# Block-sparse attention and an MLP on one core: the first pair's loads in runs of three tokens, and a new written-out order

## The chip, the cores and the metric

The kernel runs on one core of a Trainium2 chip. The metric is the device time of one execution in microseconds (us); the time given for a kernel is the median of its runs. PE is the engine of matrix products, DVE the vector engine, ACT the one of activations, POOL the general one, and SP issues most of the DMAs.

## What is computed

Four batches of 8 heads attend over 768 tokens with 64 elements per head. Each head's keys are 12 blocks of 64 tokens. A token attends to its own block and to the three blocks of its past whose mean key has the largest product with its query, causally. The heads' results, side by side, are the rows x of an MLP: 3072 rows, 512 to 2048 elements, gelu in its tanh form, and back to 512. In short (f32 in and out):

```python
k_rep = k.reshape(B, H, n_blocks, block, D).mean(axis=3)
gate_scores = np.einsum('bhsd,bhnd->bhsn', q, k_rep)        # only past and own blocks count
top_idx = np.argsort(gate_scores, axis=-1)[..., -3:]
mask = (block of key in top_idx, or own block) & (pos_q >= pos_k)
attn = softmax(where(mask, scale * q @ k.T, -1e9)) @ v
x = attn.transpose(0, 2, 1, 3).reshape(B * S, H * D)
out = gelu_tanh(x @ w_in) @ w_out
```

## The kernel before

**Staging.** Heads are worked in pairs, 16 pairs p = 0..15, four to a batch. Per batch there is an attention stage (heads) and an MLP stage: s1, the first product (L1115) with its gelu (L1127), and s2, the second (L1315 for batch 0; L1365 with sums on DVE, L1302 and L1414, in the others, which trades additions for an eighth of the products). The last batch has its first product in seven such products too (L1204). Attention of batch b + 1 is interleaved with the MLP of batch b, so that only batch 0's attention has no matrix products of an MLP beside it.

**Batch 0, a pair.** Keys and queries come in with tokens on the partitions and must be turned. `load` (L387) fetches 192 KB per head and tensor on the SP queue; the eight semaphores of DMAs go round, so that an issue can wait for the landing of an earlier one. Pair 0 has a loader of its own, `load_0` (L421): keys on the SP queue, queries on the ACT queue, four pieces of 96 KB each (half of the tokens of one head), with every token's 64 floats, 256 bytes, on another partition. `turn` makes three f32 products or transposes per half of the tokens: for pairs 0 and 1 (`KSUM`) the keys go through a product (L538) with `identk`, the identity of 128 columns with two more that hold ones for either block of a 128-token chunk, so that block sums fall out beside the turned keys; all others are transposes (L541). `turned` copies the result out of PSUM (the copies' own lines: L360 on DVE, L356 on ACT, L358 on POOL). `ksb_h` makes the sums' two-head form: from the product's extra columns by one multiplication with `bmask` (L588), or by a reduction (L576) and a multiplication (L582). The gate (L680) is four products in column strips of 32 (`tile_position`); DVE then makes the selection: transpose (L696), causal addition (L703), one max8 per group (L712), comparison (L713), and `madd`, the additive mask (L717). PE turns the mask (L749) and DVE copies it beside the queries, where it is 12 more rows of the contraction of S^T (L856: a key part of 64 rows and one with the mask's). ACT takes the exponential (L875), POOL clears what lies behind the diagonal (L901), PE multiplies with the values and a column of ones (L924), DVE divides (L942, L943), and PE turns the result into x (L981). Pair 0 has its gate in two halves, the second with `ksbx`. `cast_v` and `q16` make f16 of values and queries on POOL.

**Batches 1 to 3.** Keys and queries are transposed by DVE in 32 x 32 blocks (L557), cast to f16 (keys on DVE or POOL, queries on DVE or ACT), and the rest is as above (L1039 scores, L1052 exponential, L1066 causal, L1078 values, L961 and L962 division).

**Constants and weights.** POOL and DVE write the constants (L274 to L302, L470 to L510). POOL issues w_in as two DMAs of 1 MB (L453) once the values of pair 3 have landed (L451), then w_out. L1560 is a DMA on the SP queue that waits for w_in and holds later loads back.

**Order.** A table sets everything: each step is an `Op` with its possible engines, and `run` emits them in the list `ORDER`, on the engine that `ENGINE` names (else the first that the step lists), in the buffers that `BUFFER` deals out:

```python
for n in ORDER:
    op = self.ops[n]
    for kind, key in op.takes:
        if key not in self.buf:
            self.buf[key] = self.kinds[kind][0][next(picks)]
    op.emit(engine.get(n, next(iter(op.engines))))
```

The order in the list is the order in which each engine issues; the waits follow from the data. Steps of `warm` are products with zeros (L1517) that keep PE busy where it would stand.

Of the kernel before, what the change touches and what calls it, by code (L numbers as in the profile page):

```python
# [8 lines left out]
FP32 = mybir.dt.float32  # L9
# [219 lines left out]
def kernel(  # L229
# [9 lines left out]
    nc = tc.nc  # L239
# [1380 lines left out]
```

## Time and profile before

| | |
|---|---|
| Median of 3 runs | 253.68 us (253.64 to 253.81) |
| Profiled execution | 254.11 us |
| its span | 252.4 us |
| PE busy | 244.2 us, 97% |
| DVE, ACT, POOL busy | 188.6, 178.5, 86.8 us |
| DMA | 130927 packets, 32.62 MB, 129 GB/s over the span |
| Granted PE clock | 1.0 in all slices |
| First product of the first MLP (L1115) | at 38.40 us |

The span is what the profiler saw between first and last instruction, 1.71 us less than that execution's time. Times in the trace count from the span's start. In its rows a name is a tile or a tensor (buffer numbers left out) and the shape is partitions x elements; `DVE` behind an arrow is the engine that ended the wait. A matmul in f32 shows as two records, a transpose as one. G, XS and TS are large buffers that lend room to batch 0's loads and f16 tiles (so `G<-in_q_dram` is a load of queries, `XS<-bank` a copy of turned keys or of a mask).

### The profile page before, as it was taken

What the parts mean: (1) busy time and instruction counts of PE and PEld (TensorE: products, weight loads), DVE (VectorE), ACT (ScalarE), POOL (GpSimd) and SP (SyncE); (2) the same over time, 40 slices, a digit from 0 to 9 for tenths busy, and PEclk for the clock granted to TensorE, in tenths of its full rate; (3) what the DMA queues carried; (4) which work ended last, traced back from release to release, by engine and by line L of the source; (5) the groups of instructions that cost most, each with busy time, mean ns of one, the idle gap of its engine ahead of it and who ended that gap; (6) DMA issues with size and microseconds to landing.
All of it is one profiled execution on the core that took longest, in us unless ns stands there. A gap on an engine that the chain in (4) does not pass through costs nothing.

```text
span 252.4 us, 6423 instructions
## 1 busy us (share of the span) xinstructions
PE 244.2 (97%) x2483; PEld 170.4 (68%) x2483; DVE 188.6 (75%) x533; ACT 178.5 (71%) x225; POOL 86.8 (34%) x169
## 2 busy tenths in 40 slices
PE   7898999999999999999999999999999999999993
PEld 5665786555546666555778887656778887666883
DVE  2799863031869999999898977999775785687954
ACT  2577877546799999767899897757998927667300
POOL 8766860002135587240066644420244500000000
PEclk9999999999999999999999999999999999999999
DMA  8999599999999895999998996351601250020024
GB/s 153 219 207 184 88 211 180 214 151 160 141 153 130 155 198 93 146 176 181 167 204 145 223 154 114 88 118 42 166 4 24 41 180 20 3 84 0 4 92 158
DMA packets 130927, 32.62 MB, mean 129 GB/s; under 512 B 124528, under 2 KB 126928, under 8 KB 130896
## 3 DMA queue, kind: packets, MB, share of 16 engines
q1 hardware_dynamic: 126160, 27.62, 64.7%
q0 software_dynamic: 3136, 4.19, 10.0%
q10 hardware_dynamic: 1600, 0.39, 0.8%
q8 instruction: 19, 0.31, 0.6%
q14 instruction: 12, 0.10, 0.1%
HBM read 27.26 MB, written 6.29 MB: 133 GB/s over the span
## 4 chain that ended last, share of the span: by engine, by line
PE 91%; DVE 4%; DMA 2%; issue 1%; ACTq 1%; ACT 0%; DVEq 0%
PE wide L1115 27%; PE bank L1365 22%; PE wide L1039 11%; PE bank L1315 8%; PE bank L1078 6%; PE wide L1204 5%; PE wide L856 3%; PE bank L680 2%; PE bank L924 2%; DMA G<-in_q_dram 2%; PE bank L541 1%; PE bank L749 1%; PE bank L981 1%; DVE sel L712 1%; DVE sel L713 1%
## 5 line engine op out<-in xcount | busy, mean ns | idle before, releaser
L1115 PE MATMUL wide<-xT,w_in 128*128 128x384 f16 x416 | 74.1, 326 | 0.0
L1052 ACT ACTIVATE ats<-wide 128x896 f16<-128x896 f32 x72 | 62.0, 913 | 3.6 <-PE wide L1039 1.3
L1127 ACT ACTIVATE G<-wide 128x768 f16<-128x768 f32 x52 | 42.0, 809 | 27.0 <-PE wide L1115 25.3
L1115 PEld LDWEIGHTS <-w_in 128*128 128x128 f16 x416 | 39.9, 98 | 26.8 <-issue 1.3
L1066 POOL TENSOR_SCALAR_AFFINE_SELECT ats<-ats 128x256 f16<-128x256 f16 x72 | 31.3, 450 | 58.1 <-ACT ats L1052 57.8
L1039 PE MATMUL wide<-qT,kT 76*128 76x512 f16 (+3 forms) x192 | 38.6, 305 | 0.0
L557 DVE STREAM_TRANSPOSE s<-sd 128x768 f32<-128x768 f32 x24 | 23.2, 970 | 13.7 <-DMA sd<-in_k_dram 11.5
L1365 PE MATMUL bank<-w_out,G 128*128 128x256 f16 x216 | 31.9, 272 | 0.0
L1365 PEld LDWEIGHTS <-G 128*128 128x128 f16 x288 | 27.2, 98 | 5.2
L1315 PE MATMUL bank<-w_out,G 128*128 128x512 f16 x96 | 28.1, 379 | 0.0
L1414 DVE TENSOR_TENSOR osb<-bank,osb 128x512 f32<-128x512 f32 (+1 forms) x38 | 22.2, 594 | 7.0 <-PE bank L1365 6.5
L1039 PEld LDWEIGHTS <-kT 76*128 76x128 f16 x192 | 17.3, 97 | 10.6 <-issue 0.5
L875 ACT ACTIVATE ats<-wide 128x1024 f16<-128x1024 f32 (+3 forms) x24 | 21.0, 916 | 4.7 <-PE wide L856 4.6
L1078 PEld LDWEIGHTS <-ats 128*128 128x128 f16 x504 | 21.8, 97 | 3.6 <-POOL ats L1066 0.2
L358 POOL CAST kT<-s 64x768 f16<-64x768 f32 x23 | 19.5, 846 | 14.0 <-DVE s L557 13.2
L1078 PE MATMUL bank<-v,ats 128*128 128x65 f16 x504 | 24.1, 194 | 0.0
L1365 PEld LDWEIGHTS <-XS 128*128 128x128 f16 x216 | 20.0, 97 | 4.8
L1365 PE MATMUL bank<-TS,XS 128*128 128x256 f16 x144 | 22.8, 272 | 0.0
L358 POOL CAST v<-vsd 128x768 f16<-128x768 f32 x13 | 10.7, 828 | 30.9 <-DMA vsd<-in_v_dram 22.2
L356 ACT CAST qT<-s 64x768 f16<-64x768 f32 x21 | 17.4, 827 | 0.3
L962 DVE TENSOR_TENSOR xn<-bank,zr 128x384 f16<-128x384 f32 x24 | 13.4, 558 | 0.8
L712 DVE MAX8 sel<-sel 128x8 f32<-128x12 f32 x160 | 13.3, 157 | 0.6
(118 smaller groups left out, 350.3 us busy)
## 6 DMA issues: line engine op xcount, KB each, us to landing
out_dram<-osb SPq DMA_DIRECT2D x23, 256.0 KB
vsd<-in_v_dram SPq DMA_DIRECT2D x26, 192.0 KB
sd<-in_k_dram SPq DMA_DIRECT2D x48, 96.0 KB
sd<-in_q_dram SPq DMA_DIRECT2D x48, 96.0 KB
w_in<-in_moe_w_in_dram POOLq DMA_DIRECT2D x2, 1024.0 KB, 11.3
w_out<-in_moe_w_out_dram POOLq DMA_DIRECT2D x2, 1024.0 KB, 18.5
G<-in_q_dram SPq DMA_DIRECT2D x4, 192.0 KB
G<-in_k_dram SPq DMA_DIRECT2D x4, 192.0 KB
```

The source lines that it names most:

```text
L358: nc.gpsimd.tensor_copy(out=out, in_=in_)
L557: nc.vector.transpose(out=T[key + "T32", p], in_=T[key, p].rearrange("p t j -> p (t j)"))
L875: nc.scalar.activation(out=T["at", u][:, :, 0:n], in_=plan.buf[("st",) + u].rearrange("p (h w) -> p h w", h=2)[:, :, 0:n], func=AF.Exp, bi ...
L1039: nc.tensor.matmul(st[:, x:e], kT16[i][h][0:76, s0:s0 + 128], qT16[i][h][0:76, s0 + (x - cb):s0 + (e - cb)], start=True, stop=True)
L1052: nc.scalar.activation(out=T["at", u][:, 0:n], in_=plan.buf[("st",) + u][:, 0:n], func=AF.Exp, bias=0.0, scale=SCALE)
L1066: nc.gpsimd.affine_select(out=dg, in_=dg, compare_op=ALU.is_ge, fill=0.0, base=0, pattern=[[0, 2], [1, 128]], channel_multiplier=-1)
L1078: nc.tensor.matmul(pvv[:, qc, 0:65], at[:, cb + (qc - jc) * 128: cb + (qc - jc + 1) * 128], v16[i][:, jc, h, :], start=(gi == 0 and jc == ...
L1115: nc.tensor.matmul(hps[:, 512 * e:512 * e + HALF], w_in16[:, ci, (2 * j + e) * 128: (2 * j + e + 1) * 128], T["xT", b][:, ci, HALF * h:HAL ...
L1127: nc.scalar.activation(out=G[:, :, h, j, :], in_=plan.buf["hps", b, j, h].rearrange("p (e w) -> p e w", e=2)[:, :, 0:HALF], func=AF.Gelu_a ...
L1315: nc.tensor.matmul(plan.buf["ops", b, ti], G[:, f % 2, 2 * ti // NC, f // 2, ti % (NC // 2) * 128:ti % (NC // 2) * 128 + 128], w_out16[:, ...
L1365: nc.tensor.matmul(dst[:, HD * h:HD * h + HD], FACT[m][0][:, j, t * 128:(t + 1) * 128], FACT[m][1][:, j, :], start=(clear and j == 0), sto ...
L1414: nc.vector.tensor_tensor(out=dst(), in0=src(), in1=other(), op=ALU.add)
```

## The change

1. **Pair 0's loads.** Each partition takes three consecutive tokens of a head, one run of 768 bytes instead of three of 256. The tile is seen as `p (c h) d`, a head's half as three columns of tokens.
2. **Pair 0's turning.** A half of keys or queries is six f32 products in place of three, one per head and token column, each into 64 of the 128 output partitions (`tile_position=(0, 64 * h)`). `identk` becomes 3 x 134 columns: three identities, each with six columns that mark which block a token lies in; keys take 134 columns, queries 128. The copies put the tokens back in order (`p (w c) -> p c w`).
3. **Block sums.** `KSUM` is empty. Pair 0's sums are a reduction over the three columns of six, then the multiplication with `bmask`; pair 1's keys are now transposed, and summed by a reduction over 64 like pairs 2 and 3.
4. **Engines.** For batch 0, `cast_v`, `q16` and one kind of constants (`ones`) may run on DVE or ACT too. `ENGINE` in batch 0: the first copy of pair 0's queries, its first mask copy, both key copies of pair 1 and the first of pair 2 go from DVE to ACT, the second of pair 2 from ACT to DVE; the casts of the values of pairs 2 and 3 and the first `ones` go from POOL to DVE. Later: four key casts POOL to DVE, six query casts and three other copies ACT to DVE, all net.
5. **Order.** `ORDER` and `BUFFER` are new over the whole kernel. The numbers of useful products from batch 1 on are the same (416 of L1115, 504 of L1365, 192 of L1039, 504 of L1078); the warm-up products fall from 37 to 34. On the SP queue the first piece of pair 1's keys now stands ahead of pair 0's four pieces of keys; on the ACT queue the exponential's table load stands between the two halves of pair 0's queries. On PE the start is: queries' first half, keys' first half, keys' second half, first gate, queries' second half, pair 1's first queries, second gate, first masks (before: queries' first half, keys' first half, queries' second half, first gate, keys' second half). On DVE, pair 3's query copies now come ahead of its keys' copies and sums. On POOL the cast of pair 1's values stands ahead of the causal clearings.

The core of the diff (the lists are left out):

```diff
-    KSUM = (0, 1)
+    KSUM = ()
+    RUN = (0,)
...
-    identk = const.tile([128, 130], FP32, name="identk")
-    ident32 = identk[:, 0:128]
+    ident32 = const.tile([128, 128], FP32, name="ident32")
     make_identity(nc, ident32)
+    identk = const.tile([128, 3, 134], FP32, name="identk")
+    inblk = identk[:, :, 128:134]
+    nc.gpsimd.memset(inblk, 1.0)
+    nc.gpsimd.affine_select(
+        out=inblk, in_=inblk, compare_op=ALU.is_ge, fill=0.0, base=0,
+        pattern=[[1, 3], [-64, 6]], channel_multiplier=3)
+    nc.gpsimd.affine_select(
+        out=inblk, in_=inblk, compare_op=ALU.is_ge, fill=0.0, base=63,
+        pattern=[[-1, 3], [64, 6]], channel_multiplier=-3)
+    nc.vector.tensor_copy(out=identk[:, :, 0:128], in_=ident32.unsqueeze(1)
+                          .to_broadcast([128, 3, 128]))
...
                         (nc.sync if eng == SP else nc.scalar).dma_start(
-                            out=T[key, 0][:, 3 * a:3 * a + 3, hh, :],
+                            out=T[key, 0][:, 6 * hh + 3 * a:
+                                          6 * hh + 3 * a + 3],
                             in_=SRC[key][0, hh, HALF * a:HALF * a + HALF]
-                            .rearrange("(c p) d -> p c d", p=128))
+                            .rearrange("(p c) d -> p c d", c=3))
...
         ld["v16", p] = add(
-            {POOL: 0.85}, emit,
-            [ld["v", p], old],
+            {POOL: 0.85, DVE: 0.56, ACT: 0.84} if b == 0 else {POOL: 0.85},
+            emit, [ld["v", p], old],
...
+                    n = 134 if key == "k" else 128
+                    for h in range(2):
+                        nc.tensor.matmul(
+                            w[64 * h:64 * h + 64, c * n:(c + 1) * n],
+                            T[key, p][:, 6 * h + 3 * a + c],
+                            identk[:, c, 0:n], start=True, stop=True,
+                            tile_position=(0, 64 * h))
...
                 copy(eng, dst()[:, a * HALF:(a + 1) * HALF].rearrange(
-                    "p (c w) -> p c w", w=128),
+                    "p (w c) -> p c w" if p in RUN else "p (c w) -> p c w",
+                    c=3),
...
+                    half = slice(6 * a, 6 * a + 6)
+                    w = plan.buf["wk", p, a]
+                    nc.vector.tensor_reduce(
+                        out=ks[:, half],
+                        in_=w[:, 0:402].rearrange(
+                            "p (c w) -> p w c", w=134)[:, 128:134]
+                        if p in RUN else w[:, 0:HALF].rearrange(
+                            "p (n w) -> p n w", w=64),
+                        op=ALU.add, axis=AXL.X)
                     for x in into:
                         nc.vector.tensor_tensor(
-                            out=x[:, :, 6 * a:6 * a + 6].rearrange(
-                                "p h (c b) -> p h c b", b=2),
...
+                            out=x[:, :, half], in0=bmask[:, :, 0:6],
+                            in1=ks[:, half].unsqueeze(1).to_broadcast(
+                                [128, 2, 6]), op=ALU.mult)
...
-            q16s = ([add({POOL: 0.85}, q16(0, S), qcs, pr + 0.1)] if p else
+            q16s = ([add({POOL: 0.85, DVE: 0.56, ACT: 0.84}, q16(0, S), qcs,
+                         pr + 0.1)] if p else
                     [add({DVE: 0.33}, q16(a, HALF), [qcs[a]], pr - 0.1)
                      for a in range(2)])
```

More of the change, by code (lines that the diff above doesn't have):

```diff
@@ L382, in first @@
                     "p (t j) -> p t j", j=32))
+            if key != "v" and p in RUN:
+                T[key, p] = sd.rearrange("p c h d -> p (c h) d")
             part(0)
         def part(n):
+            if key != "v" and p in RUN:
+                nc.sync.dma_start(
+                    out=T[key, p][:, 6 * n:6 * n + 6].rearrange(
+                        "p (a c) d -> p a c d", c=3),
+                    in_=SRC[key][b, 2 * hp + n].rearrange(
+                        "(a p c) d -> p a c d", p=128, c=3))
+                return
             if not dve:
@@ L500, in consts, with emit_p @@
         for i in range(NB):
-            def emit_p(_, i=i):
-                nc.gpsimd.memset(v16[i][:, :, :, 64:65], 1.0)
-                nc.gpsimd.memset(madd[i], 0.0)
+            def emit_p(eng, i=i):
+                on = nc.vector if eng == DVE else nc.gpsimd
+                on.memset(v16[i][:, :, :, 64:65], 1.0)
+                on.memset(madd[i], 0.0)
                 if i < HP - 1:
-                    nc.gpsimd.memset(mT2[i][:, 0:128], 0.0)
+                    on.memset(mT2[i][:, 0:128], 0.0)
                 for h in range(2):
-                    nc.gpsimd.memset(qT16[i][h][64:76, 0:128], 0.0)
-            c_E["ones", i] = add({POOL: 1.3}, emit_p, [], prio=-45 + 10 * i)
+                    on.memset(qT16[i][h][64:76, 0:128], 0.0)
+            c_E["ones", i] = add({POOL: 1.3, DVE: 0.8}, emit_p, [],
+                                 prio=-45 + 10 * i)
     def fill(i, after):
@@ L534, in emit @@
                 for c in range(3):
-                    src = T[key, p][:, 3 * a + c].rearrange(
-                        "p h d -> p (h d)")
-                    if key == "k" and p in KSUM:
-                        nc.tensor.matmul(w[:, c * 130:(c + 1) * 130], src,
-                                         identk, start=True, stop=True)
-                    else:
-                        nc.tensor.transpose(w[:, c * 128:(c + 1) * 128], src,
-                                            ident32)
+                    if p not in RUN:
+                        nc.tensor.transpose(
+                            w[:, c * 128:(c + 1) * 128],
+                            T[key, p][:, 3 * a + c].rearrange(
+                                "p h d -> p (h d)"), ident32)
+                        continue
+                    n = 134 if key == "k" else 128
[5 more added lines that the diff above has]
+                            tile_position=(0, 64 * h))
             return emit
@@ L563, in pre @@
             for a in range(2):
-                t = add({PE: 0.71 if p in KSUM else 0.34}, turn("k", a),
+                t = add({PE: 0.69 if p in RUN else 0.34}, turn("k", a),
                         [ld["k", p] if p else ld["k", 0, a]], pr,
-                        takes=("pre", ("wk", p, a)))
+                        takes=("pre", ("wk", p, a)), mode=3 * (p in RUN))
                 kts.append(t)
@@ L649, in pre @@
             for a in range(2):
-                t = add({PE: 0.34}, turn("q", a),
+                t = add({PE: 0.66 if p in RUN else 0.34}, turn("q", a),
                         [ld["q", p] if p else ld["q", 0, a]], pr,
-                        takes=("pre", ("wq", p, a)))
+                        takes=("pre", ("wq", p, a)), mode=3 * (p in RUN))
                 qts.append(t)
```

33 lines of the change are left out of this document (7 added, 26 removed), and 311 rows, old and new, of tables (BUFFER, ENGINE, ORDER).

## The prediction

> **What bounds the kernel now.** I read the page's totals and its chain first, then the busy time of each engine by stage, then the timeline of the first 42 us.
>
> ```profile
> span 252.4 us, 6423 instructions
> PE 244.2 (97%) x2483; PEld 170.4 (68%) x2483; DVE 188.6 (75%) x533; ACT 178.5 (71%) x225; POOL 86.8 (34%) x169
> PE 91%; DVE 4%; DMA 2%; issue 1%; ACTq 1%; ACT 0%; DVEq 0%
> ```
>
> The profiled execution took 254.11 us, 1.71 more than its span; the median of the runs, 253.68, lies 0.43 below it. PE is busy for 97% of the span, and 91% of the chain that ended last is PE. So a gain must come from the 8 us in which PE stands still, or from PE work taken out. The stages (each row: stretch, length, then busy time and count for PE, PEld, DVE, ACT and POOL; PE's clock, DMA share, GB/s) show where those 8 us are:
>
> ```profile
> 0.00:4.70 4.70, 3.63 (x17) 2.40 (x17) 1.01 (x15) 1.49 (x2) 3.70 (x19) 1.00 0.65 131
> 4.70:7.20 2.50, 1.74 (x15) 1.35 (x14) 1.07 (x4) 0.48 (x1) 2.32 (x8) 1.00 1.35 220
> 7.20:11.00 3.80, 3.06 (x41) 2.31 (x42) 2.77 (x12) 1.31 (x3) 3.55 (x8) 1.00 1.39 218
> 11.00:31.20 20.20, 18.57 (x307) 13.73 (x303) 18.46 (x77) 16.28 (x22) 12.83 (x23) 1.00 0.94 163
> 31.20:38.40 7.20, 7.15 (x147) 5.93 (x148) 5.02 (x14) 5.76 (x8) 4.16 (x7) 1.00 1.13 212
> 38.40:60.00 21.60, 21.60 (x147) 12.87 (x145) 5.27 (x10) 12.44 (x16) 1.23 (x2) 1.00 1.21 180
> 80.00:100.00 20.00, 19.96 (x252) 12.99 (x250) 18.85 (x50) 19.72 (x26) 14.63 (x27) 1.00 0.83 141
> 122.00:156.00 34.00, 34.00 (x411) 27.61 (x409) 29.94 (x58) 31.65 (x39) 17.68 (x32) 1.00 1.02 171
> ```
>
> From 38.4 us on PE is full: a new order there can lose, hardly gain. Ahead of it PE is short of work while pair 0's data comes in (to 7.2), between the gates of pair 0's halves (7.2 to 11), and while DVE makes the selections of batch 0 one after another (18.46 of 20.20 busy). Warm-up matmuls count as busy there, so that PE's true slack is larger than its row says. What the first 38 us lose or gain the end keeps, since nothing behind them has room.
>
> **The change part by part.** *Loads and turning of pair 0, up to its first gate.*
>
> ```profile
> 2.46 4.15 DMA G<-in_q_dram
> 3.00 1.28 ACT L822 ACT_TABLE_LOAD   x1 [3.00 <-issue]
> 4.79 0.52 PE L541 MATMUL bank<-identk,G 128*128 128x128 f32 x3
> 5.15 0.83 PE L538 MATMUL bank<-identk,G 128*128 128x130 f32 x6
> 6.74 0.52 PE L541 MATMUL bank<-identk,G 128*128 128x128 f32 x3 [0.76 <-DMA G<-in_q_dram]
> 7.19 0.16 PEld L680 LDWEIGHTS bank<-s,ksb 128*32 128x32 f32 x8 [0.17 <-issue]
> 7.19 0.32 PE L680 MATMUL bank<-s,ksb 128*32 128x64 f32 x8
> 11.48 1.61 PE L538 MATMUL bank<-identk,G 128*128 128x130 f32 x12
> DMA packets 5216, 1.31 MB, mean 218 GB/s; under 512 B 5216, under 2 KB 5216, under 8 KB 5216
> GB/s 349 334 364 349 213 61 0 0 0 0 0 0 0 0 0 152 243 394 394 425 394 273 364 455 425 304 304 319 379 303 379 228 91 0 0 0 0 0 91 212
> ```
>
> The row of 5216 packets is the DMA view from 7 to 13 us: loads in 256-byte pieces run at 218 GB/s. The last row, from the same view at 247.5 to 250.2 us, is the nearest with long packets (stores): slices of 300 to 455. For 768-byte pieces I take 330, between 218 and that row's common values; the ends are 218 and 425. Pair 0's keys and queries are eight pieces of 98 KB, 786 KB: at 218 GB/s 3.6 us, and the last landed at 6.61 (2.46 + 4.15), so that data flowed from about 3.0. Afterwards the SP queue first issues a 197-KB piece of pair 1's keys in the old form (0.90 us of traffic), and the ACT queue puts the table load of 1.28 between pair 0's two halves of queries, which delays the second half but not the first. Sharing the engines evenly, the first half of queries (0.60) is in at 4.2 and that piece of pair 1 at 4.5; the two halves of keys follow at 5.1 and 5.7.
>
> A half is now turned by six products instead of three, each into half of the columns. A product in f32 shows as two records. If the two column halves run side by side, a block takes what three full ones do: 0.83 by the row at 5.15; taken 0.8. If one runs after the other, it is the row of twelve: 1.61. The gate, four column strips, eight records of 64 columns in 0.32, speaks for side by side: at the same 1.61/12 for 130 columns they would take 0.53 in turn. Afterwards PE turns the first queries (4.2 to 5.0), both halves of keys (5.1 to 5.9, 5.9 to 6.7), then the gate: 6.7 for 7.19, **-0.5**. Ends: loads at 425 GB/s and blocks of 0.7 give a gate at 6.4 (-0.8); loads at 218 with blocks of 0.8 one at 7.4 (+0.2); blocks in turn are the first rival.
>
> The Trainium skill, "TensorEngine Tiling (Array Packing)", section "Tiling Modes", has it that tiles in different columns work in parallel, but also that a change of the tiling mode drains the engine, and that column tiling shuts out the f32 transpose. By it the side-by-side value would stand, and the sum with it, less a drain at each change; the trace has 0.17 us of idle weight loading ahead of the first gate, which agrees in kind.
>
> *From the first gate to the second.*
>
> ```profile
> 9.73 0.21 DVE L717 SCALAR_TENSOR_TENSOR madd<-sel,ownm 128x48 f16<-128x48 f32 x1
> 9.86 0.16 DVE L588 TENSOR_TENSOR ksbx<-bmask,bank 128x12 f32<-128x12 f32 x1
> 10.32 0.29 DVE L360 COPY XS<-bank 128x256 f16<-128x256 f16 x1 [0.30 <-PE bank L749]
> 10.98 0.28 DVE L696 STREAM_TRANSPOSE sel<-bank 128x96 f32<-128x96 f32 x1
> ```
>
> Between the first selection and the second gate's transpose DVE makes block sums (0.16), waits 0.30 for the masks on PE, and copies the mask (0.29). The new order turns the second half of keys before the first gate, so that the sums precede the selection, and gives the mask copy to ACT: 0.16 + 0.30 + 0.29, **-0.7**. What is late next is the second gate itself, behind pair 1's first queries on PE (0.5): then -0.2, the upper end.
>
> *DVE's stretch to pair 3's selection (10.98 to 31.19).*
>
> ```profile
> 12.56 0.16 DVE L588 TENSOR_TENSOR ksb<-bmask,bank 128x12 f32<-128x12 f32 x1
> 12.63 0.55 DVE L360 CAST XS<-bank 128x384 f16<-128x384 f32 x1
> 16.45 0.55 DVE L576 TENSOR_REDUCE ks<-bank 128x6 f32<-128x384 f32 x1
> 24.34 0.17 DVE L582 TENSOR_TENSOR ksb<-bmask,ks 128x12 f32<-128x12 f32 x1
> 28.53 0.35 DVE L696 STREAM_TRANSPOSE sel<-bank 128x160 f32<-128x160 f32 x1 [0.83 <-PE bank L680]
> 30.91 0.28 DVE L717 SCALAR_TENSOR_TENSOR madd<-sel,ownm 128x120 f16<-128x120 f32 x1
> 31.11 0.55 DVE L360 COPY xT<-bank 128x768 f16<-128x768 f16 x1
> ```
>
> Out: two key copies net (1.10), and the wait of 0.83, because pair 3's query copies now precede its keys' sums. In: pair 1's two sums, 0.16 each, become a reduction and a product, 0.55 + 0.17: +1.12. Together -0.8. Pair 1's turning on PE falls from 1.61 to about 1.0, hidden behind DVE; without that cover it would be worth -0.6. New waits are likely where DVE and PE now need copies from ACT; POOL's cast of pair 1's values stands ahead of its selects and waits for that load, and the products with values queue behind them. I take 0.6 of the 0.8 for that: **-0.2**, ends -0.8 and +0.8. The cast of pair 2's values now stands on DVE between pair 3's selection and its mask copy, where the xT copy of 0.55 stood; a cast of that size takes about 0.54 (below): **0**.
>
> *ACT in batch 0.*
>
> ```profile
> 13.62 0.48 ACT L356 COPY s<-bank 128x384 f32<-128x384 f32 x1 [0.69 <-PE bank L541]
> 33.08 1.94 ACT L875 ACTIVATE ats<-wide 128x1024 f16<-128x1024 f32 x2 [0.61 <-PE wide L856]
> ```
>
> ACT takes in net three copies of about 0.48 and the mask copy. It has 3.9 us free of 20.2 up to 31.2, which covers most; behind pair 3's mask it still waits for PE (0.61). I take one copy that comes between exponentials: **+0.4**, ends 0 and +1.2 (the first three on the path, and no more room).
>
> *Weights.*
>
> ```profile
> 26.63 1.66 POOL L453 DMA_DIRECT2D w_in<-in_moe_w_in_dram  x2 [0.35 <-issue]
> w_in<-in_moe_w_in_dram POOLq DMA_DIRECT2D x2, 1024.0 KB, 11.3
> 38.40 0.65 PE wide L1115 x4
> 41.10 0.57 SPq L1560 DMA_DIRECT2D after_in<-w_in  x1
> ```
>
> The second half of w_in is there at 41.1, 13.6 after an issue at about 27.5; with a median of 11.3 for two the first took 9.0 and came at 35.6. L1115 begins at 38.4 and by the sum at 37.4, so the weights cap the gain only at 2.8. Their issue waits for pair 3's values, at the end of the same SP queue; shorter loads ahead can only bring that forward. **0**.
>
> *Batches 1 to 3.*
>
> ```profile
> L358 POOL CAST kT<-s 64x768 f16<-64x768 f32 x23 | 19.5, 846 | 14.0 <-DVE s L557 13.2
> 56.15 0.54 DVE L360 CAST kT<-s 64x768 f16<-64x768 f32 x1
> ```
>
> Four key casts go from POOL (0.85) to DVE (0.54), six query casts from ACT to DVE: 5.4 us more on DVE in all. PE's products are the same in number. With PE full this is worth nothing while DVE keeps ahead; taken **+0.2**, ends 0 and the third rival.
>
> The sum: -0.5 - 0.7 - 0.2 + 0.4 + 0.2 = -0.8; 254.11 becomes 253.3 for a profiled execution, and the median 253.68 becomes **252.9**.
>
> **The rivals.** *Column halves in turn (slower).* A block of six takes 1.61 and the queries' about 1.5; PE, not the loads, then sets the gate: 4.2 + 1.5 + 1.6 + 1.6 = 8.9, +1.7 for -0.5, and the rest of the sum as above: +1.4, 255.1. It decides when a block takes over 1.1 us: then three blocks end after 7.5 and the other terms (-0.3) are used up. Against it stands the gate's row, for it that no 64-column strip is in the trace.
>
> *ACT takes the place of DVE (no change).* All moved copies stand ahead of exponentials: +1.2 for +0.4, the gain is gone, 253.7.
>
> *The later order stalls PE (slower).* From 80 to 100 us DVE is busy 18.85 and ACT 19.72 of 20: if a third of the 5.4 us more on DVE reaches PE through late casts or sums, it is +1.8 for +0.2, in all +0.8: 254.5. For it: those rows; against: 122 to 156, where DVE has 4 us free and PE stands nowhere. It decides from 1.0 us of new idle time on PE behind 38.4.
>
> *Longer pieces gain little.* If the price is mostly by bytes, and under half of the step from 218 to 330 is had, 768 bytes run at about 267 GB/s: the keys land at 5.4 and 6.1, the gate stands at 7.0, and the sum is -0.5: 253.2. Against it only the stores' row. The Trainium skill, "DMA: Bandwidth & Descriptors", section "Why small descriptors are slow (HBM only)", gives three fixed cycles beside eight of data for 256 bytes, by which 768 bytes would need 27 in place of 33; an estimate of 18% from that page, and that 267.
>
> *All covers hold.* Loads and blocks at the good end (-0.8), the second gate -0.7, DVE's -0.8, no price on ACT or later: -2.3, 251.4.
>
> **How the numbers follow.** Forecast 0.38, all covers 0.08, little by longer pieces 0.10, halves in turn 0.12, ACT 0.12, later stalls 0.20. This kernel's runs tell about 0.2%, 0.5 us, from no change. Little by longer pieces sits at that edge and is split: faster 0.38 + 0.08 + 0.05 = 0.51, the same 0.12 + 0.05 = 0.17, slower 0.12 + 0.20 = 0.32. The range runs from all covers, 251.4, past the later stalls to 254.8, and leaves out the halves in turn and the tails, some 0.2. The likeliest case by itself spans 252.0 to 253.2.
>
> **What would show it.** Right: pair 0's pieces of 98 KB landing 0.30 apart, blocks of twelve records in 0.7 to 0.9, the first gate by 6.9, the second gate's transpose near 9.8, pair 3's selection ending about 29.8, and the first L1115 near 37.4 with PE full behind it. Wrong: blocks over 1.1; a gate after 7.5; L1115 later than 38.4; or L1115 earlier and new idle time on PE in the stages of batches 1 to 3, which the forecast puts at 0.2.

## The result: 251.94 us for 253.75

The changed kernel took 251.94 us (median of 4 runs, 251.45 to 252.62), the kernel before 253.75 beside it (4 runs): a ratio of 0.9934 with an interval of 0.9909 to 0.9958. Run again later, it took 251.74 (5 runs), 0.9918 (0.9906 to 0.9931). So the gain is 1.8 to 2.1 us. The forecast was 0.8 (252.9); the measured times lie inside its range of 251.4 to 254.8. The profiled execution is the slowest of the first four, 252.62 us with a span of 250.9.

The page of the changed kernel:

```profile
span 250.9 us, 6484 instructions
PE 245.2 (98%) x2504; PEld 170.7 (68%) x2504; DVE 194.9 (78%) x551; ACT 173.8 (69%) x220; POOL 82.2 (33%) x161
PE 94%; DVE 4%; issue 0%; DVEq 0%
```

PE's share of the chain rose from 91% to 94%. The stages of the changed kernel, with the columns of the prediction:

```profile
10.20:29.06 18.86, 18.30 (x303) 13.38 (x301) 17.69 (x78) 16.43 (x25) 11.13 (x21) 1.00 0.86 166
31.20:38.40 7.20, 7.20 (x137) 5.70 (x134) 4.68 (x12) 6.47 (x8) 4.42 (x7) 1.00 1.12 205
80.00:100.00 20.00, 20.00 (x252) 12.86 (x250) 18.38 (x48) 17.50 (x23) 13.08 (x24) 1.00 0.63 111
```

The stretch from the second gate's transpose to the end of pair 3's selection is the first row: 18.86 us, where it was 20.21 (10.98 to 31.19), with DVE busy for 17.69 and not 18.46. From 31.2 on PE has no idle time (before, 0.05 us up to 38.4). The timeline shows where the steps now lie:

```profile
4.38 3.50 PE L565 MATMUL bank<-identk,G 128*64 128x128 f32 x36
7.80 0.32 PE L699 MATMUL bank<-s,ksb 128*32 128x64 f32 x8
8.05 0.88 PE L565 MATMUL bank<-identk,G 128*64 128x128 f32 x12
8.79 0.21 DVE L722 TENSOR_TENSOR sel<-sel,cgate 128x48 f32<-128x48 f32 x1
9.45 0.21 DVE L732 TENSOR_TENSOR sel<-sel,sel 128x48 f32<-128x48 f32 x1
10.20 0.28 DVE L715 STREAM_TRANSPOSE sel<-bank 128x96 f32<-128x96 f32 x1
26.59 0.91 DVE L722 TENSOR_TENSOR sel<-sel,cgate 128x120 f32<-128x120 f32 x1
28.78 0.28 DVE L736 SCALAR_TENSOR_TENSOR madd<-sel,ownm 128x120 f16<-128x120 f32 x1
36.51 0.81 PE L1135 MATMUL wide<-xT,w_in 128*128 128x384 f16 x4
38.98 0.57 SPq L1580 DMA_DIRECT2D after_in<-w_in  x1
```

The first gate came later, at 7.80 for 7.19. All the rest came earlier: the second gate's transpose by 0.8, the end of pair 3's selection (29.06) by 2.1, the first product of the MLP by 1.7, the end of the span by 1.5. (In the timeline that product starts at 38.24 before; the 38.40 given ahead is its row in the chain, where it starts when the product ahead of it has ended.) So the loads and the turning lost time, and DVE's way through the selections won it. The same way in the kernel before holds what the prediction did not look at:

```profile
7.69 1.87 POOL L494 TENSOR_SCALAR_AFFINE_SELECT G<-G 64x768 f16<-64x768 f16 x2
7.93 0.71 DVE L703 TENSOR_TENSOR sel<-sel,cgate 128x48 f32<-128x48 f32 x1
9.11 0.51 DVE L713 TENSOR_TENSOR sel<-sel,sel 128x48 f32<-128x48 f32 x1
16.83 0.83 POOL L358 CAST v<-G 128x768 f16<-128x768 f32 x1 [2.00 <-DMA G<-in_v_dram]
17.04 0.65 DVE L582 TENSOR_TENSOR ksb<-bmask,ks 128x12 f32<-128x12 f32 x1
21.42 1.00 POOL L901 TENSOR_SCALAR_AFFINE_SELECT ats<-ats 128x256 f16<-128x256 f16 x2 [1.91 <-ACT ats L875]
21.81 0.75 DVE L713 TENSOR_TENSOR sel<-sel,sel 128x120 f32<-128x120 f32 x1
22.37 0.87 POOL L358 CAST v<-TS 128x768 f16<-128x768 f32 x1
22.66 0.72 DVE L717 SCALAR_TENSOR_TENSOR madd<-sel,ownm 128x120 f16<-128x120 f32 x1
38.24 0.81 PE L1115 MATMUL wide<-xT,w_in 128*128 128x384 f16 x4
```

These are rows of the kernel before. The first two DVE operations take 0.21 each in the changed kernel; the one at 17.04 takes 0.17 elsewhere in the same trace, the last two 0.28. Each long one stands beside a POOL operation. Nine such operations between 7 and 31 us cost the kernel before 3.4 us more than their short forms; in the changed kernel six cost 1.6. (Counted are the operations with two inputs in SBUF that take over 0.06 more than their shortest form.) The difference of 1.8 is the size of the gain, which proves nothing by itself. Theory A: POOL stretches DVE's short operations, and the new order and engines win by keeping them apart. Theory L: the loads in runs of three win. A third question, W, came from PE's rate during pair 0's turning.

### The profile page after: what moved, and what is told of

The parts are those of the page before. It is cut to its first block, busy times and chain, and to the rows that moved or that the text cites. A ratio compares the mean times of both kernels' runs of the same rounds, so it can differ in the third digit from the quotient of the medians.

```text
span 250.9 us, 6484 instructions
## 1 busy us (share of the span) xinstructions
PE 245.2 (98%) x2504; PEld 170.7 (68%) x2504; DVE 194.9 (78%) x551; ACT 173.8 (69%) x220; POOL 82.2 (33%) x161
## 4 chain that ended last, share of the span: by engine, by line
PE 94%; DVE 4%; issue 0%; DVEq 0%
PE wide L1135 27%; PE bank L1385 22%; PE wide L1059 11%; PE bank L1335 8%; PE bank L1098 6%; PE wide L1224 6%; PE wide L876 3%; PE bank L699 2%; PE bank L1537 2%; PE bank L944 2%; PE bank L1001 1%; PE bank L565 1%; PE bank L558 1%; PE bank L769 1%; DVE sel L731 1%; DVE sel L722 1%
## 5 line engine op out<-in xcount | busy, mean ns | idle before, releaser
L1135 PE MATMUL wide<-xT,w_in 128*128 128x384 f16 x416 | 75.0, 326 | 0.0
L1059 PE MATMUL wide<-qT,kT 76*128 76x512 f16 (+3 forms) x192 | 38.4, 305 | 0.0
L1385 PE MATMUL bank<-w_out,G 128*128 128x256 f16 x216 | 33.7, 272 | 0.0
L1335 PE MATMUL bank<-w_out,G 128*128 128x512 f16 x96 | 29.2, 379 | 0.0
L1098 PEld LDWEIGHTS <-ats 128*128 128x128 f16 x504 | 22.7, 98 | 4.5 <-issue 0.3
L1098 PE MATMUL bank<-v,ats 128*128 128x65 f16 x504 | 24.9, 194 | 0.0
L1385 PE MATMUL bank<-TS,XS 128*128 128x256 f16 x144 | 22.1, 272 | 0.0
L367 POOL CAST kT<-s 64x768 f16<-64x768 f32 x19 | 16.3, 862 | 9.3 <-DVE s L585 8.0
L365 ACT CAST qT<-s 64x768 f16<-64x768 f32 x15 | 12.4, 825 | 0.2
```

Of the source, the lines that this page charges most:

```text
L367: nc.gpsimd.tensor_copy(out=out, in_=in_)
L1059: nc.tensor.matmul(st[:, x:e], kT16[i][h][0:76, s0:s0 + 128], qT16[i][h][0:76, s0 + (x - cb):s0 + (e - cb)], start=True, stop=True)
L1098: nc.tensor.matmul(pvv[:, qc, 0:65], at[:, cb + (qc - jc) * 128: cb + (qc - jc + 1) * 128], v16[i][:, jc, h, :], start=(gi == 0 and jc == ...
L1135: nc.tensor.matmul(hps[:, 512 * e:512 * e + HALF], w_in16[:, ci, (2 * j + e) * 128: (2 * j + e + 1) * 128], T["xT", b][:, ci, HALF * h:HAL ...
L1335: nc.tensor.matmul(plan.buf["ops", b, ti], G[:, f % 2, 2 * ti // NC, f // 2, ti % (NC // 2) * 128:ti % (NC // 2) * 128 + 128], w_out16[:, ...
L1385: nc.tensor.matmul(dst[:, HD * h:HD * h + HD], FACT[m][0][:, j, t * 128:(t + 1) * 128], FACT[m][1][:, j, :], start=(clear and j == 0), sto ...
```

## The experiments

All times are medians beside the kernel before, which took 253.8 in each group.

**The operations by themselves.** The kernel has no part of the computation.

> This kernel leaves the whole computation out and writes zeros; it has five stages. In each DVE runs the operations of a selection five times over, alone (stage 1), beside ACT copies (2), beside POOL's causal selects (3), beside POOL's casts (4) and beside POOL's memsets (5); at the end of each stage PE, idle until then, runs a train: 40 pairs of f32 products in column halves (1), 40 full f32 products (2), 40 full f16 products (3), 15 full f16 and then 40 pairs in column halves (4), 15 full f16 and then 40 full f32 (5). Theory A (POOL's work stretches DVE's short operations): the additive, comparing and multiplying operations that read only SBUF take 0.17 to 0.28 in stages 1 and 2 and 0.5 to 0.9 in stages 3 and 4, while the transpose, the reduction and the copy out of PSUM and the max8 stay at 0.34, 0.55, 0.55 and 0.16 in all. Rival: the long ones seen in the traces come from ACT, DMA or data, and all stages agree within 0.05. For PE: if column halves are slow by themselves, pairs are 0.21 apart through all of stage 1 and in stage 4, and full products 0.11 per record; if PE only starts slowly, every train begins at twice its later distance for about 3.5 us, whatever its form, and stage 4's column halves, after 3.2 us of full products, run at 0.11 per pair.

It was executed once. The groups by line of DVE follow: first the stage with nothing beside it (4.2 to 19.7 us), then beside POOL's selects (40.9 to 58.6), beside its casts (64 to 79) and beside its memsets (82.6 to 98.2):

```profile
L89 DVE CAST o<-src 128x384 f16<-128x384 f32 x5 | 1.8, 360 | 0.2
L78 DVE SCALAR_TENSOR_TENSOR madd<-sel,own 128x120 f16<-128x120 f32 x5 | 1.4, 283 | 0.2
L75 DVE TENSOR_TENSOR sel<-gm,mx 128x120 f32<-128x120 f32 x5 | 1.4, 283 | 0.2
```

```profile
L78 DVE SCALAR_TENSOR_TENSOR madd<-sel,own 128x120 f16<-128x120 f32 x5 | 3.2, 646 | 0.2
L68 DVE TENSOR_TENSOR gm<-gx,cg 128x120 f32<-128x120 f32 x5 | 1.8, 368 | 0.2
```

```profile
L78 DVE SCALAR_TENSOR_TENSOR madd<-sel,own 128x120 f16<-128x120 f32 x3 | 2.6, 855 | 0.1
L89 DVE CAST o<-src 128x384 f16<-128x384 f32 x4 | 2.3, 580 | 0.1
L75 DVE TENSOR_TENSOR sel<-gm,mx 128x120 f32<-128x120 f32 x3 | 1.5, 503 | 0.1
L66 DVE STREAM_TRANSPOSE gx<-src_ps 128x160 f32<-128x160 f32 x4 | 1.3, 334 | 0.0
L74 DVE MAX8 mx<-gm 128x8 f32<-128x12 f32 x9 | 1.0, 161 | 0.1
```

```profile
L89 DVE CAST o<-src 128x384 f16<-128x384 f32 x4 | 2.8, 691 | 0.1
L75 DVE TENSOR_TENSOR sel<-gm,mx 128x120 f32<-128x120 f32 x5 | 1.4, 283 | 0.2
```

The mean ns is the second number behind the bar. Operations with two inputs in SBUF go from 283 to as much as 646 beside selects (the comparison, L75, only to 294, less than theory A expected) and to 503 to 855 beside casts; beside memsets they stay at 283. The cast from SBUF goes from 360 to 580 beside casts and, beside memsets, to 691. The transpose out of PSUM (341 alone) and the max8 (161) do not move. ACT copies (second stage) changed nothing. Theory A's mechanism is shown; what it is worth in the kernel is not shown by it. The Trainium skill, "SBUF — State Buffer", section "Who interferes with whom", says that a DVE instruction with two SBUF inputs contends with a POOL instruction that reads SBUF, not with one that only writes; the 283 beside memsets agrees.

For PE, the starts of the products in that trace: every train began at half rate, whatever its form (0.21 to 0.22 from one product of 256 f16 columns, or one record or pair of 134 f32 columns, to the next), for 4.8 us (column halves), 6.1 (full f32), 3.6 (full f16), and 4.0 and 3.5 (f16 first). Then a pair of column halves is 0.11 from the next, as one record of a full product is. Column halves run side by side and are not slow by themselves. Two rows of that kernel's page, 40 slices of 2.84 us, show PE's busy tenths and the tenths of its clock that were granted:

```profile
PE   4200000899923999900029900000099996079996
PEclk9999999999997559997555997555557999967999
```

The second train, full f32 products, fills the slices from 36.9 to 48.2 us, the 14th to the 17th. In the first two of them the clock reads 5, in the next two 9, and the half rate ended at 42.1. So the half rate is the granted clock. For the first train, at 20.16, the row reads 9 all the same: the trace's first record of the clock begins at 25.0, where that train's half rate ended, and ahead of the first record the view shows full speed.

**The two halves of the change.** First the changed kernel with the old `ORDER`, `BUFFER` and `ENGINE`:

```diff
-ORDER, BUFFER, ENGINE of the changed kernel
+ORDER, BUFFER, ENGINE of the kernel before
```

> The changed kernel with the order, the buffers and the engines of the kernel before: runs of three tokens, column halves, block sums by reduction for pair 1, all in the old places. Theory A (the gain comes from the order and the engines, which keep POOL away from DVE's selections): no gain; pair 0 is turned in 1.1 us a block and pair 1's sums cost DVE 1.1 us more, so 254.0 to 255.5. Theory L (the gain comes from the loads of pair 0): most of it is there, 252.0 to 252.8.

Measured: 255.59, ratio 1.0074 (1.0056 to 1.0091). Then the old loads, products and sums under the new lists (`ones` able to run on DVE):

> The kernel before (256-byte pieces, three products a block, pair 1's sums by PE) with the order, the buffers and the engines of the changed one. Theory A: most of the gain stays, 251.5 to 252.6; the first gate comes later than 7.8 us because pair 0's pieces stand behind a piece of pair 1's keys at 218 GB/s, but DVE's stretch from the second gate to pair 3's selection is 18.5 to 19 us as in the changed kernel. Theory L: no gain, 253.5 to 254.5.

Measured: 254.24, 1.0014 (1.0001 to 1.0028). Neither half has the gain: +1.8 and +0.4 alone, -1.8 to -2.1 together. Theory L is refuted as put. Of theory A the first expectation came true (a little above its 255.5, and with blocks of 0.81, not 1.1), the time of the second did not; yet in the second kernel's profile DVE's stretch from the second gate's transpose to pair 3's selection is 18.4 us (11.15 to 29.55), as theory A expected (20.21 in the kernel before). But the selection's end, 1.6 earlier than in the kernel before, is 0.6 at the first product of the MLP (37.61) and 0.4 at its twentieth, and PE loses 0.7 behind that. Timeline of the first of the two:

```profile
4.75 2.42 PE L555 MATMUL bank<-identk,G 128*64 128x128 f32 x36
8.25 1.86 POOL L504 TENSOR_SCALAR_AFFINE_SELECT G<-G 64x768 f16<-64x768 f16 x2
8.51 0.69 DVE L722 TENSOR_TENSOR sel<-sel,sel 128x48 f32<-128x48 f32 x1
9.32 0.85 DVE L726 SCALAR_TENSOR_TENSOR madd<-sel,ownm 128x48 f16<-128x48 f32 x1
```

Here the three blocks of pair 0 took 2.42, 0.81 each, and the first gate stood at 7.10. In the old places the new loads met the same POOL selects, on other operations (0.69 and 0.85 for 0.21 each), and pair 1's gate, which now waits for DVE's sums, came 1.6 later (15.14 for 13.52). In the second kernel, PE's own rows:

```profile
5.48 0.88 PE L534 MATMUL bank<-identk,G 128*128 128x128 f32 x3 [1.02 <-DMA G<-in_q_dram]
6.14 2.83 PE L531 MATMUL bank<-identk,G 128*128 128x130 f32 x12
8.91 0.44 PE L673 MATMUL bank<-s,ksb 128*32 128x64 f32 x8
```

PE stood for 1.02 between warm-up products and the first queries, turned twelve records at half rate in 2.83 (twelve take 1.61 at full rate in the kernel before), and reached the gate at 8.91. Its clock's first record begins only at 9.78. The same kernel with five more warm-up products:

```diff
 ORDER: 15 warm-up products, then pair 0's first queries
+ORDER: 20
```

> The old loads and products in the new order, as before (254.24), with five more warm-up products at the start, so that PE is not idle before the first queries land at 5.3. That kernel turned pair 0 at half rate to 9.7 us and had its first gate at 8.9. Theory W: full rate from 4.7 on, first gate at about 7.4, and 1.0 to 1.8 us of the time gone: 252.5 to 253.2. What is then left between it and 251.94 is the worth of the new loads and sums as such. Rival (the new order needs the new loads): the time stays within 0.4 of 254.24.

Measured: 253.90, 1.0010 (0.9993 to 1.0027). Its profile has the first gate at 8.05, full rate from 6.1, the end of pair 3's selection at 29.42, 1.8 earlier than in the kernel before, and the first product of the MLP at 36.88, 1.4 earlier. But that execution, 253.15, is the fastest of ten, and the median is no better than the kernel before. By the times this is the rival's case, that the new order needs the new loads; what holds the slower executions was not profiled.

**The start.** Two more warm-up products in the changed kernel:

```diff
 ORDER = [...,
-    1904, 71,
+    1904, 1924, 1925, 71,
```

> The changed kernel with two more warm-up products at the start, 17 in place of 15, as the kernel before has. In the changed kernel's trace the turning of pair 0 starts at 4.38 and runs at half rate to 6.84 (0.21 us a pair of column halves, 0.11 later); the stages by themselves show that PE, from idle, runs at half rate for 3.5 us under full f16 products and 4.8 to 6.1 under f32 ones. Theory W (two warm-ups too few cost pair 0's turning half of PE's rate): the turning starts at 4.73 at full rate, waits only for the pieces of keys, and the first gate moves from 7.80 to 7.0 to 7.2; if DVE's chain behind it holds, the kernel takes 251.2 to 251.6 for 251.94. Rival (column halves or the loads hold the gate): the gate stays at 7.8 or moves back by 0.35, and the time is 251.9 to 252.3. Third: the gate moves, but the time does not, because PE is full from 13 us on: 251.8 to 252.1.

Measured: 251.93, 0.9936 (0.9915 to 0.9958): nothing gained. The turning began at 4.81 and still ran at half rate, to 6.4; the gate stood at 7.81. Theory W fell: with the same 17 warm-up products full rate came at 4.6 in the kernel before and in the one with the new loads in the old order, and at 6.5 here. The number of warm-ups does not set it. The changed kernel unedited:

> The changed kernel once more, unedited, on this chip and beside these runs, for a narrower interval and a second profile. 251.4 to 252.4, as in its first four runs (251.45 to 252.62). If the half-rate period at PE's start differs between executions of the same program, it ends elsewhere than at 6.84 here, with the start of the first product at 1.07 again.

Its timeline beside the first profile's 3.50 and 7.80:

```profile
4.38 2.95 PE L565 MATMUL bank<-identk,G 128*64 128x128 f32 x36
7.26 0.32 PE L699 MATMUL bank<-s,ksb 128*32 128x64 f32 x8
26.27 0.28 DVE L722 TENSOR_TENSOR sel<-sel,cgate 128x120 f32<-128x120 f32 x1
35.60 0.81 PE L1135 MATMUL wide<-xT,w_in 128*128 128x384 f16 x4
```

Same program, same start, but the half rate ended at 5.7 in place of 6.8 (the clock's first record begins at 5.76 and at 6.97), the gate came 0.54 and the first product of the MLP 0.9 earlier, and this execution took 251.74 for 252.62. The period differs between executions. It is not what made most of the difference: of the 0.54 only 0.2 was left at the second gate's transpose (10.00 for 10.20). The other 0.7 came in DVE's stretch behind it. There pair 3's causal addition took 0.28 for 0.91, because the POOL cast that it had met in the first profile began at 26.81, after it. All long operations together cost 0.8 here and 1.6 there. With one program and one order, this speaks for theory A.

**POOL and DVE in the changed kernel.** Three steps back on POOL:

```diff
 ENGINE:
-    "DVE": [2, 56, 61],   # ones of pair 0, casts of the values of pairs 2 and 3
```

> The changed kernel with the casts of the values of pairs 2 and 3 and the first set of ones back on POOL. Theory A: each POOL cast of 0.83 that meets a short DVE operation which reads only SBUF stretches it by 0.4 to 0.5; with one or two such meetings on the way to pair 3's selection, less the 0.56 that DVE saves behind that selection, 252.1 to 252.8. Rival (DVE gains what it gives up, PE waits for neither): 251.7 to 252.1.

Measured: 252.84, 0.9960 (0.9945 to 0.9976), 0.9 to 1.1 more than the changed kernel. Its timeline:

```profile
28.32 0.82 POOL L358 CAST XS<-s 128x768 f16<-128x768 f32 x1
28.34 0.95 DVE L727 SCALAR_TENSOR_TENSOR madd<-sel,ownm 128x120 f16<-128x120 f32 x1
```

A cast of values now stands ahead of POOL's issue of w_in, which comes 1.8 later than in the first profile (26.61 for 24.84; 1.73 of idle time ahead of it has no cause in the profile). Behind it the cast of pair 3's queries comes late and stands beside the last operation of pair 3's selection: 0.95 for 0.28. The cast of values itself meets a multiplication at 23.99: 0.66 for 0.17. The number lies at the upper end of theory A's 252.1 to 252.8. The reverse, one cast out of the way:

```diff
 ORDER (POOL):
-    231, 242, 157, 145, 265,
+    231, 145, 242, 157, 265,   # 145: cast of pair 3's queries; the rest selects, 157 w_in
```

> The changed kernel with one step moved on POOL: the cast of pair 3's queries, which runs from 26.55 to 27.37 beside pair 3's selection (its causal addition takes 0.91 for 0.28), is issued ahead of pair 1's last causal select, near 23.3. Theory A: the addition is 0.28 again, pair 3's selection ends 0.4 to 0.6 earlier than 29.06, and the time falls to 251.4 to 251.7. Rival (a select that is late by 0.8 holds PE's products with pair 1's values, or PE is full there anyway): 251.9 to 252.3.

Measured: 252.02, 0.9932 (0.9910 to 0.9954). The addition took 0.28 and the selection ended at 28.62, but pair 3's gate came at 25.85 where variants that differ elsewhere have it at 25.5; the time did not move. The long operations of that trace still cost 1.5 in all: other ones met POOL instead. Inconclusive. Taken together, the profiled executions of the changed kernel and of the three variants so far (two more warm-ups, casts on POOL, this one) took 251.74, 252.19, 252.22, 252.62 and 252.86, and their long operations cost 0.8, 1.1, 1.5, 1.6 and 2.0. The two rise together, which agrees with theory A but is no proof.

The same idea in the kernel before, constants alone:

```diff
 ORDER (POOL):
-    5, 2, 0, 3, 1, 4, 202     # 1: table for the mask's rows; 0: gate tables; 2..5: ones of pairs 0..3
+    1, 0, 202, 4, 5           # 202: the first causal select
 ENGINE:
+    "DVE": [2, 3]
```

> The kernel before with POOL's constants out of the way of pair 0's first selection and nothing else: the mask table first, the ones of pairs 0 and 1 on DVE, idle there, and the ones of pairs 2 and 3 behind POOL's first causal select. In the trace of before two operations of that selection stand beside POOL's selects of that table (7.69 to 9.56) and take 0.71 and 0.51; the same operations take 0.21 each in the changed kernel, where POOL is idle. Theory A: they take 0.21 here too, the masks come 0.6 to 0.8 earlier than 9.94, and of that 0.4 to 0.8 arrives at the end: 253.0 to 253.4 for 253.8. Rival (the second half's queries on PE and ACT hold the second gate anyway): the selection is shorter but the second gate stays at 10.5 and the time within 0.2 of 253.8.

Measured: 253.47, 0.9984 (0.9968 to 1.0001). Its timeline, of an execution of 252.47:

```profile
7.72 0.21 DVE L696 TENSOR_TENSOR sel<-sel,cgate 128x48 f32<-128x48 f32 x1
8.39 0.21 DVE L706 TENSOR_TENSOR sel<-sel,sel 128x48 f32<-128x48 f32 x1
9.54 0.37 PE L673 MATMUL bank<-s,ksbx 128*32 128x96 f32 x8
```

The two operations are short, the second gate is a whole 1.0 earlier (9.54 for 10.54), the MLP 1.7 (36.56 for 38.24); the long operations cost 1.3 in all, for 3.4. But of ten runs five took 252.3 to 253.2 and five 253.8 to 254.1; what parts them is open, so this gain is not settled by the median. The kernel before has two such groups too: 7 of its 70 runs beside the experiments took 252.7 to 253.2, the others 253.5 or more. No execution of its quicker group was profiled.

**The later order.** The changed kernel to the first products of the MLP, then the lists of the kernel before:

```diff
-ORDER[254:], with its buffers and engines
+what is left, in the order of the kernel before, with its buffers and engines
```

> The changed kernel up to the first product of the MLP's first stage (36.5 us), then the order, buffers and engines of the kernel before for all that is left. Both theories place the gain ahead of 36.5 us: 251.6 to 252.2, no more than 0.3 from the changed kernel's 251.94, with the first product of that stage at 36.5. Rival (the later order brings part of it): 252.6 to 253.5.

Measured: 253.03, 0.9974 (0.9963 to 0.9986), 1.1 to 1.3 more than the changed kernel. The rival's number, but not its cause:

```profile
39.49 1.46 PE L1126 MATMUL wide<-xT,w_in 128*128 128x384 f16 x8 [0.94 <-ACT G L1138]
```

At the seam both PSUM buffers of the first stage wait for a gelu, and PE stands for 0.94 that neither kernel has. Its twentieth product of that stage is at 41.59, 0.3 ahead of the kernel before (41.90), and so is the end of its span (252.1 for 252.4): behind the seam the old order keeps what it was given. In the changed kernel it is at 40.42, 1.5 ahead, and the span ends 1.5 ahead too. By these profiles the later order is worth nothing either way, within 0.2; the 1.2 lost in this execution was lost at the seam. All other traces of the whole kernel say the same, whichever the order: from the twentieth product to the end they take 210.3 to 210.6, but for 211.2 with the old loads in the new order. The first 42 us decide the time, as the prediction had it.

**Fillers.** The chain of the changed kernel has warm-up products of L1537 on it between 13 and 37 us. Without the 19 later ones:

```diff
-ORDER: 1905 to 1923, between the first gate and the MLP
```

> The changed kernel with its first 15 warm-up products only; the 19 that lie between 8.9 and 36.5 us are left out. They are on the chain that ended last in eleven places, some 2 us of it in all. If they only cost (PE keeps its full rate without them): 250.0 to 251.0. If PE would stand there anyway: 251.7 to 252.2. If PE falls back to half rate where it now idles for longer: over 253.

Measured: 251.18, 0.9900 (0.9885 to 0.9916), 0.6 less than the changed kernel in the same group; the intervals just overlap. PE kept its rate. Of the stretch from 11.0 to 31.2, the first row is this kernel's:

```profile
11.00:31.20 20.20, 19.03 (x343) 14.18 (x340) 18.69 (x79) 18.01 (x25) 13.40 (x25) 1.00 0.89 173
```

and the second the unedited kernel's, second profile:

```profile
11.00:31.20 20.20, 20.01 (x350) 14.71 (x348) 18.97 (x78) 18.21 (x25) 13.23 (x25) 1.00 0.86 171
```

PE's 20.01 of 20.20 was partly fillers: with them gone it has 1.2 free, and the MLP starts at 35.35 for 35.60. This is the fastest version of all. How much of the 0.6 the fillers themselves cost is not settled: in this execution the long DVE operations cost 0.4, in the unedited one 0.8. On top of it, pair 1 loaded and turned as pair 0 is:

```diff
-    RUN = (0,)
+    RUN = (0, 1)
```

> The changed kernel without its 19 later fillers (251.18) and with pair 1 loaded and turned as pair 0 is: runs of three tokens, column halves, sums from the six added columns. If the loads set the pace up to 19 us, as the chain of the kernel without fillers has it, pair 1's 786 KB come about 1.0 us sooner, DVE's sums of pair 1 fall from 0.72 to 0.35 each, and the four blocks of pair 1 cost PE 0.33 more each, in time that the fillers held: 250.2 to 250.9. Rival (PE is the bound from 13 us on): four times 0.33 come on top: 251.6 to 252.5.

Measured: 251.78, 0.9926 (0.9912 to 0.9940). The rival's number: PE is busy for 20.05 of those 20.20 again, 1.0 more than without pair 1's blocks.

## Why the prediction was right

The sign was right and the times fell inside the range. The size was less than half of what came (0.8 for 1.8 to 2.1), and three of the five terms were well off: one was a loss that was forecast as a gain, two were gains much larger than forecast. That the time came as near as it did is in part luck.

- **Turning of pair 0, -0.5; measured +0.6** (7.80 for 7.19), or +0.1 in the second profile (7.26). Two steps failed. One is the loads: the first queries landed at 4.21, for 4.2, but the two halves of keys at 5.57 and 6.15, for 5.1 and 5.7. The DMA view from 2.4 to 6.4 us, these pieces and pair 1's, has slices of 177 to 372 GB/s and 274 on average, not 330; this is nearly the rival that gave little to longer pieces (267, keys at 5.4 and 6.1). The other is the price of a block, 0.8: thirty-six records took 3.50, 1.17 a block. Not because halves run in turn (at full rate a pair of halves takes 0.11, as one full record does), but because PE ran at half rate to 6.8. The row of 0.83 came from a stretch in which PE was already at full rate. There the price holds: 0.81 a block with the new loads in the old order, and 0.81 from the start of a later block, at 8.05, to the next product. In the first profile PE's rate set the gate, since both halves of keys had landed before PE came to them. In the second, where full rate came at 5.7, PE began the keys at 5.72, just after their landing at 5.66.
- **First gate to second, -0.7; measured -1.4** (2.40 from gate to transpose for 3.79). The three pieces named went, and beside them 0.8 from the two operations that POOL had stretched, less 0.25 because the sums now precede the first selection's transpose (0.64 behind the gate, for 0.39). The prediction quoted one selection's end and not its inside.
- **DVE's stretch, -0.2; measured -1.35.** Count by count the exchange was right: sums for copies, and the 0.83 wait at pair 3's gate gone. The 0.6 set aside for new waits was not needed: DVE's idle time fell from 1.75 to 1.17; and its busy time fell by 0.77, which the exchange, even at +0.02, cannot give. That is collisions again: in this stretch they cost 2.6 before and 1.6 after.
- **ACT, +0.4; measured +0.4.** From the end of pair 3's selection to the first product of the MLP 7.45 (29.06 to 36.51) for 7.05 (31.19 to 38.24). That it is copies between exponentials was not looked at.
- **Weights, 0.** Right: the second half of w_in was there at 38.98 for 41.10 and nothing waited for it.
- **Batches 1 to 3, +0.2.** The first twenty products of the MLP cost 0.25 more (3.91 for 3.66), as they are interleaved with others; from there to the end both kernels take 210.5. DVE and PE in the row from 80 to 100 us say the same: 18.38 and 20.00.

In the profiles of the kernel before and of the first execution after, the terms add up to the change of the span: +0.6 - 1.4 - 1.35 + 0.4 + 0.25 = -1.5. Two of the prediction's own signs of being wrong came, blocks over 1.1 and a gate after 7.5, and the time fell all the same: the forecast 0.8 was the sum of a loss and a gain that it did not see.

The rivals: halves in turn is refuted by the 0.11 for a pair. Little by longer pieces was nearly right about the loads, but not about the time (253.2), which DVE's way decided. ACT in DVE's place wanted +1.2 where 0.4 was measured. The later order was to leave PE idle behind 38.4; from there to the end it costs nothing. "All covers hold" (251.4) is the nearest to what happened, for another reason. What would have shown it beforehand: in the trace of before, the same operation has two durations, 0.28 and 0.75; every such pair is a question, and the answer stands in POOL's rows at the same time.

What stays open: how much of 1.8 the collisions are, since the two halves of the change do not add; what parts the two groups of runs, with moved constants and in the kernel before; and how much of the difference between the two halves is the phase of PE's clock at the start, which is one draw in each profile.

## What to carry to other kernels

Before costing an engine's chain by its rows, sort the rows of one operation and shape by duration: where the longest is over twice the shortest, look at what the other engines did at that moment, and price the move of that work, not only the chain. A load format, the order around it and the places of other engines' work are one choice: tried apart, one half of this change loses 1.8 and the other gains nothing. And a filler is work: take it out once the order is set, and see whether it still fills anything.

## What the hardware showed that was not expected

- DVE operations with two SBUF inputs take 0.28 alone, up to 0.65 beside POOL selects and 0.86 beside POOL casts; the same beside POOL memsets take 0.28. The f32 to f16 cast out of SBUF is stretched by memsets too (0.36 to 0.81).
- PE starts at half rate for 3.5 to 6.1 us of products, differently in two executions of one program (to 5.7 and to 6.8, both from 1.07). It is the granted clock: it read 0.50 in such a stretch of the operations by themselves. In the kernels the view shows 1.00 from the start, because the first record of the clock begins where the half rate ends (4.63 before, 6.97 and 5.76 after). The Trainium skill, "TensorE: Matmul & The Clock Gate", section "Part 1: The HAM clock gate (the "warmup" mystery)", puts this down to an activity window of 3.4 us that runs freely, with the change varying by half a microsecond from run to run. The trace agrees with the window: in the operations by themselves the clock's changes, from 25.02 to 103.53 us, lie 3.41, 6.83, 10.24, 13.66 or 17.06 us apart, whole multiples of 3.41. The spread here was larger, 1.2 us in the same program.
- Loads in 256-byte pieces from two queues ran at up to 286 GB/s (view of the kernel before, 2.4 to 6.8 us), from the SP queue alone at 218. But the 286 were gone at 4 us, while the ACT queue's packets ran to 5.8: from 4.0 to 5.6 both queues together moved 198 to 235. So the second queue is not shown to be the reason. With pair 0 in 768-byte pieces the average was 274 (2.4 to 6.4 us), before 236 (2.4 to 6.8).
